# Retention and a gated feed-forward on one core: k's last heads on another queue, casts set among the steps, eight v buffers, and earlier loads

## The chip, the cores and the metric

The kernel runs on one core of a Trainium2 chip. The metric is the device time of one execution in microseconds. The kernel before was timed three times: 336.51 is the median, 334.05 the lowest and 338.14 the highest. One more execution was recorded by the hardware profiler; every row shown is from that one.

## The reference

Two stages follow each other, the first giving the second its rows:

```python
scores = (1 / sqrt(D)) * q @ k.T                     # per batch and head: 8 x 8, S = 576, D = 64
Dmat = where(i >= j, gamma[h] ** (i - j), 0)         # gamma[h] = 1 - 2 ** (-5 - h)
x = (scores * Dmat) @ v                              # then heads side by side: 4608 rows of 512
h = x @ w_in                                         # 512 -> 2048
out = (h * tanh(softplus(h))) @ w_out                # 2048 -> 512
```

All inputs and the output are float32 in memory; the kernel multiplies in bf16.

## The kernel before

The 576 positions of a batch are cut into four chunks of 128 and one of 64; the last chunks of two batches share one. That gives 36 chunks of 128 rows, and four chunks make a tile of 512 rows, nine tiles in all. The first two tiles hold the first chunk of each of the eight batches, which needs no earlier state. The other 28 chunks need the scores within the chunk and the sum of all earlier k and v, the state, which is carried per batch.

The order of the work is written out by hand: the scheduler is off, and each engine runs its instructions in the order in which the program states them. So an instruction that waits holds everything behind it on its engine. VectorE, ScalarE, GpSimd (POOL in the profile) and TensorE are four such rows; SyncE (SP), ScalarE and POOL also issue the loads. A DMA issue on a queue waits, besides for its buffer, for a semaphore that was last used eight loads before.

*Tile 0* (`f_cast(0, p)`, `f_transpose(0, p)`, `f_scores(0, p)`, `f_v(0, b)`, `f_out(0, b)`). A pair p is two of the eight heads. q is loaded in float32 into `stage`, a tile of the later type gT that is still free, by SP (heads 0 to 4) and ScalarE; k is loaded by POOL (`load_first_k`, L105), which casts on the way, into `kb0`; v by SP (L117). VectorE casts q pair by pair (L185), TensorE transposes q and k (L196), ScalarE copies them out (L200), TensorE makes the scores (L210), and VectorE multiplies them with the decay into the upper half of `stage` (L215). v is cast by POOL and ScalarE (L221). TensorE then gives the output (L235), which VectorE and ScalarE copy to xT (L238).

*The weights* come by POOL: w_in in two loads of 256 columns and three of 512 (L86), w_out in four (L89).

*Tile 1's q and k* are loaded by SP (`load_second_qk`, L112) into both halves of `stage`, pair by pair, q before k, sixteen loads of 128 KB. VectorE casts both (L185, two instructions a pair). All eight casts stand on VectorE ahead of the steps that follow.

*Tile 0's first feed-forward half* is `g1(0, f)`, f from 0 to 15: four matmuls of 128x512 (L369) and the activation on ScalarE (L371). Its second half, `g2_first`, sixteen groups of four matmuls (L395), is interleaved with tile 1's attention by a table: at step i, the letters T (transpose, L196, copies by VectorE for q and ScalarE for k, L200), S (scores), V (cast of v, ScalarE) and O (output) are run for pair or batch n, then one group. The tables before and after are in the change below. q's copy and k's copy of one pair read the same tile, and k's waits for q's.

*State scaling.* `f_state(t, b)` is a POOL multiplication of a first chunk's v with the inverse decay (L244), eight in all. `load_k0(b)` loads a first chunk's k once more, in the layout that the state needs (L248).

*From tile 2 on*, `load(n)` gives a chunk's q, k and v to POOL's queue (L262, or L266 for a shared chunk). The letters are P (VectorE scales q, L272), V (POOL scales v, L278), T (transposed by TensorE, or from chunk 16 on by SP's DMA, L290), S (scores, L300, and their mask, L304) and O (L350 and L355, copied by L359). `state` is L332, copied by L336. Tile 2's attention lies among the 24 steps of a loop over u that runs `g1(1, u)` and the first eight steps of `g2(1, ...)`, four steps to each j = u // 4; the others lie in the loop over t and i. `g2` is L384. Buffers for q and v in tiles 2 and later rotate over five (`io`, bufs = PF = 5), v with tile 0's and tile 1's v among them.

Of the kernel before, what the change touches and what calls it, by code (L numbers as in the profile page):

```python
# [10 lines left out]
F32 = mybir.dt.float32  # L11
# [6 lines left out]
def kernel(  # L18
# [18 lines left out]
    nc = tc.nc  # L37
    B, H, S, D = q.shape
    assert (B, H, S, D) == (8, 8, 576, 64)
    P = 128  # L40
    NP = H // 2
    d_model = H * D
    d_ff = moe_w_in.shape[1]
    nF = d_ff // P
    KC = d_model // P
    NCH = 4
    NPE = 16
    PF = 5
# [11 lines left out]
    N0 = 2 * NCH  # L60
# [4 lines left out]
    io = ctx.enter_context(tc.tile_pool(name="io", bufs=PF))  # L65
# [19 lines left out]
    def load_w_in(f0, n):  # L85
        nc.gpsimd.dma_start(out=w_in_t[:, :, ds(f0, n)], in_=w_in_r[:, :, ds(f0, n)])  # L86

    def load_w_out(i):
        nc.gpsimd.dma_start(out=w_out_t[:, ts(i, 4), :], in_=w_out_r[:, ts(i, 4), :])  # L89
# [2 lines left out]


    stage = gp.tile([P, nF, NCH * P], BF16, name="gT")
    raw = {0: (stage[:, 0:H, :].bitcast(F32),)}
    v0 = {}

    def rows(x, t, h):
        return x[ds(4 * t, 4), h, 0:P, :].rearrange("b (g r) d -> g b (r d)", r=4)
# [3 lines left out]
    def load_first_k(hs):  # L103
        for h in hs:
            nc.gpsimd.dma_start(out=kb0[:, h, :], in_=rows(k, 0, h))  # L105
# [7 lines left out]

    def load_first_v(t):
        for b in range(4 * t, 4 * t + 4):
            v0[b] = io.tile([P, H, D], F32, name="vraw")
            (nc.gpsimd if t else nc.sync).dma_start(out=v0[b], in_=v[b, :, 0:P, :].rearrange("h p d -> p h d"))  # L117

    for h in range(H):
        (nc.sync if h < 5 else nc.scalar).dma_start(out=raw[0][0][:, h, :], in_=rows(q, 0, h))  # L120
    load_first_v(0)

    zeros = consts.tile([P, 512], BF16)
# [13 lines left out]
                   allow_small_or_imprecise_dtypes=True)  # L137
    nc.gpsimd.iota(pos[64:P, 4:5], pattern=[[1, 1]], base=512, channel_multiplier=1,
                   allow_small_or_imprecise_dtypes=True)
    load_first_k(range(2, H))  # L140
    lg = [math.log(1.0 - 2.0 ** (-5.0 - h)) for h in range(H)]
    ex = consts.tile([P, 5, H], F32)
    for h in range(H):
# [26 lines left out]
    def keep_warm(n):  # L170
        for _ in range(n):
            nc.tensor.matmul(idle, lhsT=zeros[:, 0:P], rhs=zeros, start=True, stop=True)
# [5 lines left out]
    fst = {}  # L178

    def f_cast(t, p, copies):  # L180
        if p == 0:
            fst[t] = {"qb": first.tile([P, H, 4 * D], BF16, name="qb"),
                      "kb": first.tile([P, H, 4 * D], BF16, name="kb") if t else kb0, "vb": {}}
        for copy, name, src in zip(copies, ("qb", "kb"), raw[t]):
            copy(fst[t][name][:, ds(2 * p, 2), :], src[:, ds(2 * p, 2), :])  # L185

    def f_transpose(t, p, copies):
        if t == 0:
# [30 lines left out]
    def f_v(t, b, copy):  # L219
        vb = first.tile([P, H, D], BF16, name="vb", bufs=4)  # L220
        copy(vb, v0[4 * t + b])  # L221
        fst[t]["vb"][b] = vb
# [17 lines left out]
    def f_state(t, b):  # L240

        n = 4 * t + b
        v0s[n] = first.tile([P, H, D], BF16, name="v0s", bufs=B)
        nc.gpsimd.tensor_tensor(v0s[n], v0[n], gv[:, 0, :].unsqueeze(2).to_broadcast([P, H, D]), op=OP.mult)  # L244

    def load_k0(b):
        k0[b] = first.tile([P, H, D], BF16, name="k0", bufs=B)
        nc.gpsimd.dma_start(out=k0[b], in_=k[b, :, 0:P, :].rearrange("h p d -> p h d"))  # L248
# [3 lines left out]
    def load(n):  # L252
        if n >= n_chunks:
            return
        b, c = chunks[n]
        qr = io.tile([P, H, D], F32, name="qraw")
        vr = io.tile([P, H, D], F32, name="vraw")
        qks = io.tile([P, 2, H, D], BF16, name="qks", bufs=9)
        live[n] = {"q": qr, "v": vr, "qks": qks}
        for t, src in ((qr, q), (qks[:, 1], k), (vr, v)):  # L260
            if c < 4:
                nc.gpsimd.dma_start(  # L262
                    out=t, in_=src[b, :, ds(P * c, P), :].rearrange("h p d -> p h d"))
            else:
                for e in range(2):
                    nc.gpsimd.dma_start(  # L266
                        out=t[ds(64 * e, 64)],
                        in_=src[b + e, :, ds(512, 64), :].rearrange("h p d -> p h d"))
# [153 lines left out]
    def att(n, steps):  # L422
        if n >= n_chunks:
            return
        for step in steps:
            {"P": step_p, "V": step_v, "T": step_t, "S": step_s, "O": step_o}[step](n)

    dve, act, pool = nc.vector.tensor_copy, nc.scalar.copy, nc.gpsimd.tensor_copy


    for p in range(NP):
        f_cast(0, p, (dve,))
    keep_warm(8)
    for p in range(NP + 1):
        if p < NP:
# [3 lines left out]
            f_scores(0, p - 1)  # L439
    nc.scalar.activation(warm, pos[:, 0:1], AX.Mish)  # L440
    f_v(0, 0, pool)
    f_v(0, 1, pool)
    load_w_in(0, 256)
    load_w_in(256, 256)
    f_v(0, 2, pool)
    f_v(0, 3, act)
    for i in range(1, 4):
# [3 lines left out]
    load_second_qk()  # L451
    for i in range(4):
        load_w_out(i)
    for b in range(4):
        f_state(0, b)
    load_first_v(1)
    load_k0(0)
    make_masks()
    nc.vector.tensor_scalar(gq, gq, 1.0 / math.sqrt(D), None, op0=OP.mult)


    for p in range(NP):
        f_cast(1, p, (dve, dve))
    for f in range(nF):
        g1(0, f)
    load(N0)
    steps = {0: "T0", 1: "T1", 3: "S0", 4: "S1", 5: "T2", 8: "S2 T3", 11: "S3",
             12: "V0 V1 V2 V3", 13: "O0", 14: "O1 O2", 15: "O3"}
    for i in range(nF):
        for step in steps.get(i, "").split():  # L470
            n = int(step[1])
            if step[0] == "T":
                f_transpose(1, n, (dve, act))
            elif step[0] == "S":
                f_scores(1, n)
            elif step[0] == "V":
                f_v(1, n, act)
            else:
                f_out(1, n, (dve, act)[n % 2])
        g2_first(i // 4, i % 4)  # L480
    for b in range(4):
        f_state(1, b)
        if b == 1:
            load_k0(1)
        load(N0 + 1 + b)


    att(N0, "PV")
    for u in range(24):
        j, w = divmod(u, 4)  # L490
        if w == 0:
            if j < 3:
                load_k0(2 * j + 2)
                load_k0(2 * j + 3)
            if 0 < j:
                att(N0 + j, "PV") if j < 5 else None
                load(N0 + j + PF - 1) if j < 5 else None
            if 2 <= j < 6:
                att(N0 + j - 2, "O")
        elif w == 3 and j < 4:  # L500
            att(N0 + j, "T")
        elif w == 1 and 1 <= j < 5:
            att(N0 + j - 1, "S")
            state(N0 + j - 1)
        elif w == 2 and j < 5:
            state(N0 + max(j - 1, 0))
        if u < nF:
            g1(1, u)
        else:
            g2(1, u - nF)  # L510
    queued = [3 * NCH + PF]

    def more_loads(upto):
        for _ in range(2):
            if queued[0] <= upto:
                load(queued[0])
                queued[0] += 1

    for t in range(2, nT + 1):
        for i in range(nF):  # L520
            n, w = NCH * (t + 1) + i // 8 * 2, i % 8
            if t == nT:
                pass
            elif n == 3 * NCH:
                steps = {0: ((n, "T"), (n + 1, "PV")), 1: ((n + 1, "T"), (n, "K")),
                         3: ((n, "S"), (n + 1, "S"), (n + 1, "K")), 2: ((n + 2, "PV"),), 4: ((n + 3, "PV"),),
                         6: ((n + 1, "K"), (n, "O"), (n + 1, "O"), (n + 3, "K"), (n + 2, "T")),
                         7: ((n + 3, "T"),)}
                for m, step in steps.get(w, ()):
                    if step == "K":  # L530
                        state(m)
                        continue
                    att(m, step)
                    if step == "PV":
                        more_loads(m + PF)
            else:
                if w == 0:
                    att(n, "S")
                    att(n + 1, "S")
                    state(n + 1)  # L540
                if w in (0, 2):
                    att(n + 2 + w // 2, "PV")
                    more_loads(n + 2 + w // 2 + PF)
                elif w in (1, 3):
                    att(n + 2 + w // 2, "T")
                elif w == 4:
                    state(n + 3)
                    att(n, "O")
                    att(n + 1, "O")
                    state(n + 3)  # L550
                elif w == 6:
                    state(n + 3)
            if t < nT:
                g1(t, i)
            if t == 2:
                if i % 2:
                    g2(1, 8 + i // 2)
            elif t < nT or i < 12:
                g2(t - 1, i)
# [31 lines left out]
```

## Time and profile before

| | |
|---|---|
| median of 3 runs (lowest, highest) | 336.51 us (334.05, 338.14) |
| profiled execution, its time | 334.8 us |
| its span, from first to last instruction | 333.1 us |
| granted TensorE clock, mean over the span | 0.974 |
| busy: TensorE, weight loads, ScalarE, POOL, VectorE | 94%, 46%, 41%, 43%, 34% |
| first L369 of tile 0, of tile 1 | 19.65 us, 61.48 us |
| moved by DMA | 44.42 MB, mean 133 GB/s |

Times in rows count from the span's start. A row of the timeline gives start, duration, engine, line, operation and tiles; in square brackets stands how long the engine was idle before it and what ended that. "Busy" of TensorE counts matmuls from start to a modelled end, so it hides small gaps. DMA issues have their own view: how many, of what size, and the median time from issue to landing.

### The profile page before, as it was taken

What the parts mean: (1) busy time and instruction counts of PE and PEld (TensorE: products, weight loads), DVE (VectorE), ACT (ScalarE), POOL (GpSimd) and SP (SyncE); (2) the same over time, 40 slices, a digit from 0 to 9 for tenths busy, and PEclk for the clock granted to TensorE, in tenths of its full rate; (3) what the DMA queues carried; (4) which work ended last, traced back from release to release, by engine and by line L of the source; (5) the groups of instructions that cost most, each with busy time, mean ns of one, the idle gap of its engine ahead of it and who ended that gap; (6) DMA issues with size and microseconds to landing.
All of it is one profiled execution on the core that took longest, in us unless ns stands there. A gap on an engine that the chain in (4) does not pass through costs nothing.

```text
span 333.1 us, 5965 instructions
## 1 busy us (share of the span) xinstructions
PE 313.2 (94%) x2464; PEld 151.8 (46%) x2464; DVE 113.8 (34%) x160; ACT 137.8 (41%) x253; POOL 144.8 (43%) x178
## 2 busy tenths in 40 slices
PE   6889769999999999999969999999999999999995
PEld 2444324455445545444524444545454544444444
DVE  2641254354344342424251152525242432000111
ACT  5636213766276535342413433434344432333300
POOL 7593352999998856263708053627210000000000
PEclk9959979999999999999978999999999999999999
DMA  7999999999999999695999359798450400010031
GB/s 171 180 180 245 241 222 116 247 191 166 171 218 198 115 190 169 123 188 99 95 167 186 70 112 174 118 168 134 76 123 28 100 33 31 33 31 31 33 89 69
DMA packets 82490, 44.42 MB, mean 133 GB/s; under 512 B 65184, under 2 KB 74144, under 8 KB 82464
## 3 DMA queue, kind: packets, MB, share of 16 engines
q0 software_dynamic: 48336, 25.17, 56.5%
q1 hardware_dynamic: 33552, 18.36, 25.2%
q10 hardware_dynamic: 576, 0.52, 0.6%
q8 instruction: 19, 0.31, 0.4%
q14 instruction: 7, 0.06, 0.1%
HBM read 38.80 MB, written 9.44 MB: 145 GB/s over the span
## 4 chain that ended last, share of the span: by engine, by line
PE 78%; DMA 14%; DVE 3%; ACT 1%; issue 1%; POOL 1%; SPq 1%; DVEq 0%; ACTq 0%; POOLq 0%
PE hp L369 32%; PE ops L384 28%; DMA qkT<-qks 7%; DMA gT<-in_k_dram 6%; PE sc L300 2%; PE st L332 2%; PE hp L384 2%; PE hp L395 2%; DMA kb<-in_k_dram 2%; PE st L395 1%; ACT ssb L336 1%; PE sc L350 1%; PE hp L406 1%; PE sc L287 1%; PE sc L355 1%
## 5 line engine op out<-in xcount | busy, mean ns | idle before, releaser
L369 PE MATMUL hp<-xT,w_in_t 128*128 128x512 bf16 x576 | 147.8, 387 | 0.7 <-ACT xT L238 0.7
L371 ACT ACTIVATE gT<-hp 128x512 bf16<-128x512 f32 x144 | 86.1, 598 | 127.5 <-PE hp L369 125.7
L384 PE MATMUL ops<-w_out_t,gT 128*128 128x512 bf16 x464 | 118.9, 381 | 0.3 <-DVE res L414 0.3
L369 PEld LDWEIGHTS <-w_in_t 128*128 128x128 bf16 x576 | 54.1, 99 | 63.9 <-issue 5.4
L384 PEld LDWEIGHTS <-gT 128*128 128x128 bf16 x496 | 48.5, 98 | 59.5 <-issue 2.9
L414 DVE COPY res<-ops 128x512 f32<-128x512 f32 x30 | 20.8, 692 | 147.9 <-PE ops L384 144.4
L262 POOL DMA_DIRECT2D qraw<-in_q_dram x24 | 22.3, 930 | 53.8 <-DVE qks L272 51.9
L304 DVE TENSOR_TENSOR sm<-sc,mask 128x1024 bf16<-128x1024 f32 x28 | 33.2, 1217 | 12.4 <-PE sc L300 12.4
L278 POOL TENSOR_TENSOR vs<-vraw,gv 128x512 bf16<-128x512 f32 x28 | 30.4, 1098 | 12.4 <-PE sc L355 12.4
L336 ACT ACTIVATE ssb<-st,diag 128x256 bf16<-128x256 f32 x64 | 26.8, 470 | 17.1 <-PE st L332 16.3
L262 POOL DMA_DIRECT2D vraw<-in_v_dram x24 | 21.8, 907 | 9.0 <-ACT vb L221 6.7
L262 POOL DMA_DIRECT2D qks<-in_k_dram x24 | 21.7, 904 | 2.8 <-DMA w_out_t<-in_moe_w_out_dram 2.8
L359 DVE CAST xT<-sc 128x512 bf16<-128x512 f32 x28 | 18.2, 686 | 11.7 <-PE sc L355 11.6
L272 DVE TENSOR_TENSOR qks<-qraw,gq 128x512 bf16<-128x512 f32 x28 | 18.1, 683 | 0.0
L300 PE MATMUL sc<-qkT 64*128 64x128 bf16 x224 | 9.6, 221 | 3.3 <-DMA qkT<-qks 3.2
L350 PE MATMUL sc<-qkT,ssb 128*64 128x128 bf16 (+1 forms) x256 | 11.2, 215 | 0.0
L300 PEld LDWEIGHTS <-qkT 64*128 64x128 bf16 x224 | 6.4, 95 | 10.4 <-issue 5.9
L355 PE MATMUL sc<-sm,vs 128*64 128x128 bf16 x224 | 10.9, 219 | 0.0
L288 ACT COPY qkT<-sc 128x1024 bf16<-128x1024 bf16 x8 | 8.1, 1010 | 6.0 <-PE sc L287 5.9
L266 POOL DMA_DIRECT2D qraw<-in_q_dram x8 | 5.7, 714 | 11.3 <-DVE qks L272 11.3
L350 PEld LDWEIGHTS <-ssb 128*64 128x64 bf16 x256 | 7.8, 111 | 2.5 <-issue 2.5
L200 ACT COPY kbT<-sc 128x512 bf16<-128x512 bf16 x4 | 2.3, 585 | 16.0 <-DVE qbT L200 16.0
(81 smaller groups left out, 195.1 us busy)
## 6 DMA issues: line engine op xcount, KB each, us to landing
out_dram<-res SPq DMA_DIRECT2D x31, 256.0 KB, 3.2
vraw<-in_v_dram POOLq DMA_DIRECT2D x28, 256.0 KB, 6.7
qraw<-in_q_dram POOLq DMA_DIRECT2D x24, 256.0 KB, 5.8
qks<-in_k_dram POOLq DMA_DIRECT2D x24, 128.0 KB, 6.4
w_out_t<-in_moe_w_out_dram POOLq DMA_DIRECT2D x4, 512.0 KB, 22.1
gT<-in_q_dram SPq DMA_DIRECT2D x13, 128.0 KB, 7.4
w_in_t<-in_moe_w_in_dram POOLq DMA_DIRECT2D x3, 512.0 KB, 10.5
vraw<-in_v_dram SPq DMA_DIRECT2D x4, 256.0 KB, 7.2
```

The lines of the kernel that those rows point to most:

```text
L262: nc.gpsimd.dma_start(out=t, in_=src[b, :, ds(P * c, P), :].rearrange("h p d -> p h d"))
L272: nc.vector.tensor_tensor(live[n]["qks"][:, 0], live[n]["q"], gq[:, c, :].unsqueeze(2).to_broadcast([P, H, D]), op=OP.mult)
L278: nc.gpsimd.tensor_tensor(vs, live[n]["v"], gv[:, c, :].unsqueeze(2).to_broadcast([P, H, D]), op=OP.mult)
L300: nc.tensor.matmul(sc[:, e, p, :], lhsT=qk[r, 1, p, :], rhs=qk[r, 0, p, :], start=True, stop=True)
L304: nc.vector.tensor_tensor(sm.rearrange("p e n i -> p (e n) i"), sc.rearrange("p e n i -> p (e n) i"), m.unsqueeze(1).to_broadcast([P, 2 * ...
L336: nc.scalar.activation(ssb[:, :, e, :], st, AX.Copy, scale=diag[:, e:e + 1])
L350: nc.tensor.matmul(ot[ds(64 * e, 64), p, ds(i0, iw)], lhsT=st_sb[bb, cc][:, p, e, :], rhs=qk[:, 0, p, ds(i0, iw)], start=(i0 == 0 and p == ...
L359: nc.vector.tensor_copy(xts[t][:, :, ts(s, P)], ot)
L369: nc.tensor.matmul(hp, lhsT=w_in_t[:, c, ts(f, P)], rhs=xts[t][:, c, :], start=(c == 0), stop=(c == KC - 1))
L371: nc.scalar.activation(gts[t][:, f, :], hp, AX.Mish)
L384: nc.tensor.matmul(ops, lhsT=gts[t][:, f, ts(s, P)], rhs=w_out_t[:, f, :], start=(f == 0), stop=(f == nF - 1))
L414: copy(ot, ops)
```

## The change

- Heads 6 and 7 of tile 0's k leave POOL's queue. SP loads them in float32, ahead of tile 0's v, into the part of `stage` that pair 3's scores will take, and POOL casts them into `kb0`.
- The first 512 columns of w_in come in one load, between POOL's first and second cast of v.
- The v tiles rotate over eight buffers.
- Tile 1's v and the first `load_k0` go ahead of tile 0's state scaling; between the four scalings stand the loads of tile 2's chunks 8 to 11. They were issued after `g1(0)` and beside tile 1's scalings. Tile 1's scalings go into the loop over u, and chunks 12 to 15 are loaded behind them.
- Tile 1's casts of pairs 2 and 3 move into the table of steps, as letter C; S2 moves from step 8 to step 9.
- `load_k0` of batches 1 to 7 is spread: 1 before the loop over u, 2 and 3 at its end, 4 to 7 at steps 4 and 12 of tiles 3 and 4.

```diff
-    raw = {0: (stage[:, 0:H, :].bitcast(F32),)}
+    raw = {0: (stage[:, 0:H, :].bitcast(F32), stage[:, H:nF, :].bitcast(F32))}
...
-            v0[b] = io.tile([P, H, D], F32, name="vraw")
+            v0[b] = io.tile([P, H, D], F32, name="vraw", bufs=8)
...
+    for h in (6, 7):
+        nc.sync.dma_start(out=raw[0][1][:, h, :], in_=rows(k, 0, h))
     load_first_v(0)
...
-    load_first_k(range(2, H))
+    load_first_k(range(2, 6))
...
-            copy(fst[t][name][:, ds(2 * p, 2), :], src[:, ds(2 * p, 2), :])
+            if copy is not None:
+                copy(fst[t][name][:, ds(2 * p, 2), :], src[:, ds(2 * p, 2), :])
...
-        vr = io.tile([P, H, D], F32, name="vraw")
+        vr = io.tile([P, H, D], F32, name="vraw", bufs=8)
...
-        f_cast(0, p, (dve,))
+        f_cast(0, p, (dve, pool if p == 3 else None))
...
     f_v(0, 0, pool)
+    load_w_in(0, 512)
     f_v(0, 1, pool)
-    load_w_in(0, 256)
-    load_w_in(256, 256)
...
+    load_first_v(1)
+    load_k0(0)
     for b in range(4):
         f_state(0, b)
-    load_first_v(1)
-    load_k0(0)
+        load(N0 + b)
     make_masks()
...
-    for p in range(NP):
-        f_cast(1, p, (dve, dve))
+    f_cast(1, 0, (dve, dve))
+    f_cast(1, 1, (dve, dve))
     for f in range(nF):
         g1(0, f)
-    load(N0)
-    steps = {0: "T0", 1: "T1", 3: "S0", 4: "S1", 5: "T2", 8: "S2 T3", 11: "S3",
+    steps = {0: "T0", 1: "T1", 3: "S0 C2", 4: "S1", 5: "T2", 6: "C3", 8: "T3", 9: "S2", 11: "S3",
              12: "V0 V1 V2 V3", 13: "O0", 14: "O1 O2", 15: "O3"}
...
+            elif step[0] == "C":
+                f_cast(1, n, (dve, dve))
...
-    for b in range(4):
-        f_state(1, b)
-        if b == 1:
-            load_k0(1)
-        load(N0 + 1 + b)
+    load_k0(1)
...
-            if j < 3:
-                load_k0(2 * j + 2)
-                load_k0(2 * j + 3)
-            if 0 < j:
-                att(N0 + j, "PV") if j < 5 else None
-                load(N0 + j + PF - 1) if j < 5 else None
+            if 0 < j < 5:
+                att(N0 + j, "PV")
+                f_state(1, j - 1)
+                load(N0 + j + 3)
+            if j == 5:
+                load_k0(2)
+                load_k0(3)
...
-    queued = [3 * NCH + PF]
+    queued = [4 * NCH]
...
+            if t in (3, 4) and i in (4, 12):
+                load_k0(2 * t - 2 + i // 8)
```

## The prediction

> **What bounds the kernel now.** I read the page first, then TensorE's waits, then the timeline around the longest one.
>
> ```profile
> PE 313.2 (94%) x2464; PEld 151.8 (46%) x2464; DVE 113.8 (34%) x160; ACT 137.8 (41%) x253; POOL 144.8 (43%) x178
> ...
> PEclk9959979999999999999978999999999999999999
> ```
>
> TensorE is busy 94% of the span, so no other engine can be the bound on average; what can be won is its idle time and the slices where its clock is below 9. Those are slices 3, 5 and 6 (17 to 25 us, 33 to 50 us) and a pair past the middle. TensorE's waits say why:
>
> ```profile
> PE sc L210 <- ACT kbT L200: 4.8, 1, 4.8
> PE sc L300 <- DMA qkT<-qks: 3.2, 1, 3.2
> PE hp L196 <- DVE qb L185: 1.9, 1, 1.9
> ```
>
> Columns: total us, how often, the longest. The first row is one wait of 4.8 us before tile 1's first scores (L210). The timeline there, start and duration in us:
>
> ```profile
> 37.10 0.41 PE L196 MATMUL sc<-ident,qb 128*64 128x128 bf16 x8
> ...
> 38.55 1.03 PE L395 MATMUL ops<-w_out_t,gT 128*128 128x512 bf16 x4
> ...
> 40.32 0.43 DVE L185 CAST qb<-gT 128x512 bf16<-128x512 f32 x1 [1.81 <-DMA gT<-in_q_dram]
> 42.57 0.43 DVE L185 CAST kb<-gT 128x512 bf16<-128x512 f32 x1 [1.83 <-DMA gT<-in_k_dram]
> 42.92 1.28 DVE L200 COPY qbT<-sc 128x512 bf16<-128x512 bf16 x2
> 43.69 1.18 ACT L200 COPY kbT<-sc 128x512 bf16<-128x512 bf16 x2 [7.42 <-DVE qbT L200]
> ...
> 44.33 0.61 PE L210 MATMUL sc<-qbT,kbT 64*128 64x128 bf16 x8 [4.76 <-ACT kbT L200]
> 44.87 1.89 PE L395 MATMUL st<-w_out_t,gT 128*128 128x512 bf16 x4
> ```
>
> The transposes of pairs 0 and 1 had been done since 37.5. Their copies (L200) sat on VectorE behind the casts of pairs 2 and 3, which wait for SyncE's q and k loads, the last landing at 42.5. The wait is one of order on VectorE, not of data that TensorE needs then. And it costs more than itself, as the windows show (columns: busy of PE, PEld, DVE, ACT, POOL; granted clock; DMA share; GB/s):
>
> ```profile
> 42.00:44.00 2.00, 0.00 (x0) 0.00 (x0) 1.43 (x3) 0.31 (x1) 0.88 (x1) 1.00 1.24 233
> 44.00:46.00 2.00, 1.67 (x11) 0.78 (x12) 1.22 (x2) 0.86 (x2) 0.16 (x1) 0.56 1.09 258
> 46.00:48.00 2.00, 2.00 (x13) 0.69 (x12) 0.86 (x2) 0.00 (x0) 1.99 (x3) 0.59 1.08 209
> ```
>
> After the idle stretch the clock is near half until 47.6: from the scores at 44.33 to the transposes of pair 2 at 48.39 pass 4.06 us; the same two score groups (0.33 each, from 51.66 to 51.98) and two groups of four L395 (0.97 each) take 2.60 at full clock. So 1.46 us more.
>
> **The change, part by part.** *Casts of pairs 2 and 3 among the steps.* Nothing is removed; four casts of 0.43 go behind the first scores' multiply (C2) and behind T2 (C3). I follow the new order, with the durations above. TensorE ends its third L395 group at 39.57 and starts S0 there (its kbT copy would be ready at 37.6). VectorE: the multiply starts 0.44 after S0 and takes 1.23, so to 41.24; C2 to 42.10 (its data landed by 38.0); S1's multiply to 43.33; T2's qbT copy 0.69, to 44.02; C3 to 44.88 (its data landed by 42.5). TensorE: T2 at 39.57 + 2.60 = 42.17, just past C2; three L395 groups (0.97, 0.86, 0.86) and T2's own 0.57 bring T3 to 45.43, 0.55 past C3. So no wait of size is left: 0, at worst 1.0 (C2 caught by one POOL scaling of 1.1, less the 0.07). S2 one step later costs one more change between short and long matmuls, 0.1 (a group of four takes 0.97 after one, 0.86 otherwise). Part: -4.76 - 1.46 + 0.1 = -6.1. What is late next: T3, when pair 3's k lands after 43.0.
>
> *Two heads of k on SyncE ahead of v; their cast on GpSimd.* Removed: two L105 issues (0.59 each on POOL). Added: two 128 KB loads on SP ahead of four v loads, and one GpSimd cast, taken as its v cast of the same shape, 0.61. The last q load on SP lands at 9.3 (issued 3.73, 5.6 to landing), the second v at 12.8 (5.02 + 7.8): k's heads 6 and 7 lie between, and I take 10.9, since a q load follows the one before by 0.6 to 1.6. Cast until 11.6; TensorE needs it at 12.86. At 12.8 it would cost 0.6. The v casts follow: v moves up to 1.6 back, and the first weight load waits behind the first v cast on POOL. But TensorE starts L369 only at 19.65:
>
> ```profile
> 13.39 1.49 POOL L86 DMA_DIRECT2D w_in_t<-in_moe_w_in_dram  x2
> ...
> 15.43 2.24 POOL L86 DMA_DIRECT2D w_in_t<-in_moe_w_in_dram  x3
> ...
> 20.57 4.11 POOL L244 TENSOR_TENSOR v0s<-vraw,gv 128x512 bf16<-128x512 f32 x4
> ```
>
> *One 512-column weight load for two of 256.* Removed: one issue of 0.76. The pair landed at 17.2 and 19.9 (3.8 and 5.7 after issue), so a half takes 2.6 once the queue runs and 1.2 to start; the next 512 columns landed 3.2 later. One such load alone is then 1.2 + 3.2 = 4.4. Issued at 12.9, estimated from a first v at 12.3 and its cast, it is there at 17.3. Bounds: 16.7 if that v is no later and the cast of k alone holds it, 20.2 if it moves as two halves (1.2 + 5.2) and 0.9 later. I take the middle, so 0; worst 0.6. With the 0.6 before and 0.3 for later weights this part is 0, from -0.5 (a first landing of k sooner, as the queue is two loads lighter) to +1.5.
>
> *Loads ahead of the state scaling, eight v buffers.* The 4.11 us of L244 no longer stand before tile 1's v loads. That brings little: each of these issues waits for the eighth load before it on POOL's queue, as the 0.7 to 3.2 us idle before L117, L248 and L262 show, and the queue is fed all the while (245 GB/s from 24 to 40 us). SP's loads had 117 GB/s of it (eight loads of 128 KB in 8.97) and should keep them: 0. The last v of tile 1 landed at 50.2; its ScalarE cast is needed at 54.1 now. Eight buffers end the 6.7 us that POOL waited at L262 for ScalarE's v casts; loads of chunks 9 to 11 follow at once, 9 landing about 55.3 to 57 (chunk 8's v at 54.25, then 1.0 per 256 KB), needed from 59.3. Behind them on POOL stand the masks: 4 scalings x 1.05 and 12 issues x 0.9 put them at 58 to 59.4; VectorE's first use is 67.2 - 6.1 = 61.1. Covered by 1.7; without that cover S8's multiply and, after 1.7 more, O8 are late one for one. Later, each chunk's load runs one chunk less ahead; chunk 12's q is issued at 63.6 (masks at 59.4, a k load, two vs and one state scaling), lands 5.8 later at 69.4 and is multiplied at 72.7 (78.8 before). The k loads of batches 4 to 7 move from 72 to 79 us (with two that go to the end of the loop over u, 70 to 79 in all) into tiles 3 and 4, 0.9 of POOL each, where POOL idles (51.9 us before L262 in all). All 0, worst +1.
>
> [...] First the row: the scaling of gq (L459), 128x40, took 2576 ns at 19.19, ending with the first L244 scaling at 21.7, where ex (L144) took 175 for 128x5; yet the cast at 31.31 took its usual 0.43 beside a v issue from 31.27 on. [...] By the rows alone no scaling lies beside C2 or C3, and it stays -6.1.
>
> **Sum.** Profiled execution 334.8 (span 333.1 and 1.7 around it) - 6.1 = 328.7. The median of the runs shown, 336.51, lies 1.7 above that execution, the lowest 0.75 below; I forecast half of the 1.7 on top, 329.6.
>
> **Rivals.** *The second wait goes too, or comes again.* TensorE's other wait, 3.2 at L300, stands on a DMA transpose that took 14.0 to land where the median is 6.1:
>
> ```profile
> 168.00:171.60 3.60, 0.39 (x11) 0.22 (x12) 1.82 (x2) 0.00 (x0) 0.00 (x0) 0.85 1.07 143
> 171.50:177.50 6.00, 5.98 (x22) 2.32 (x23) 2.43 (x3) 0.70 (x2) 3.21 (x4) 0.51 1.20 195
> ```
>
> Its price is 3.2 idle and 6.00 x 0.49 = 2.9 at half clock, 6.1. The change does not touch that transpose; if the slow landing was chance and stays away, 329.6 - 6.1 = 323.5. For: one in 20 transposes. Against: the runs shown are no lower than the profiled one by more than 0.75.
>
> *Slower: the moved k loads beside the transposes.* Tiles 3 and 4 now get four POOL loads more on the engines that carry these transposes. A transpose has 14.0 - 3.2 = 10.8 us before TensorE waits. From one extra landing beyond that on, the gain is gone (335.7); with two it is 329.6 + 12.2 = 341.8. Against: a k load of 128 KB moved a landing by 0.4 to 0.9 at 75 to 77 us, and 6.1 + 0.9 is far from 10.8.
>
> *The wait moves to T3 or the weights.* If POOL's queue takes two thirds of the rate instead of half, pair 3's k lands near 46 and T3 starts 1.5 to 3 late, with some half clock: 332 to 335. For: margins of 0.07 and 0.55 only. Against: the equal share from 24 to 42 us, with POOL's queue never empty before either.
>
> *It does not do what it says:* the order on VectorE does change, so only a missed landing as above could undo it; with the first stage's worst, 335.6.
>
> **Chances.** Forecast 0.62; both waits gone 0.12; moved to T3 or the weights 0.14 (half of it still under 333.1); undone 0.04; slower 0.08. A measurement of this kernel tells about 1%, 3.4 us, from no change. Faster by over 1%: 0.62 + 0.12 + 0.06 = 0.80; within 1% 0.12; slower 0.08. The range 325.0 to 334.5 leaves out the slower case and most of the lowest; the forecast's own, the parts' ends and 2 for the spread of the runs shown, is 327 to 333.
>
> **What would show it.** Right: no wait of scores on kbT in TensorE's waits (L213 on L203 then), clock 9 in slices 5 and 6, tile 1's first L372 near 55.4 where L369 stood at 61.48, tile 0's still near 19.65, C3's k cast ending before T3. Wrong: TensorE waiting for casts (L188) or w_in_t, masks after 61, transposes landing past 10.8, or a gap of the same size at tile 1's V and O steps.

## Result, and the profile after

The changed kernel takes 324.73 us (median of four runs, 323.80 to 325.27) beside 337.09 for the kernel before (334.05 to 338.14): a ratio of 0.9645, with a 95% interval from 0.9576 to 0.9713. It is faster by some 12 us. Ratios, here and below, are of the runs' means and leave out runs that fell into a slower state (1.5% above the fastest of the same kernel), so they need not equal the quotient of two medians. The forecast of 329.6 had the direction right and missed the size; the time lies 0.3 below the range's low end of 325.0.

The profiled execution took 324.53 us against 334.8. In the code the lines behind the start have moved by 3: L369 is now L372, L395 is L398, L300 is L303, L332 is L335, the copies of the results L417 and their stores L420.

From the page of the kernel after, the busy times and the granted clock in 40 slices:

```profile
PE 308.4 (96%) x2464; PEld 150.3 (47%) x2464; DVE 111.3 (34%) x160; ACT 138.1 (43%) x253; POOL 143.8 (45%) x176
...
PEclk9879999799999999999999999999999999999999
```

The dips at 33 to 50 us and past the middle are gone. One is new, in slice 8 (56 to 65 us). TensorE's waits in the same trace (total us, how often, longest):

```profile
PE st L335 <- DMA qks<-in_k_dram: 2.3, 1, 2.3
PE hp L199 <- DVE qb L188: 2.2, 1, 2.2
PE st L238 <- DVE gT L218: 1.5, 2, 0.9
```

Both waits that headed this list before, 4.8 for kbT and 3.2 for the transposed q and k, are gone. A new one of 2.3 stands at the top.

The ledger, from the starts of the first-half groups in both traces, before minus after: the first group of tile 0 starts 0.61 sooner (19.65 to 19.04); the clock comes up 0.80 sooner behind it; from there to tile 1's first group 6.18 are won (it starts at 53.89 instead of 61.48); in tile 1's first four groups 4.00 are lost (8.25 us instead of 4.25); 0.31 are won up to tile 4; and 6.26 in tile 4. The sum is 10.16, and the last group is 10.15 sooner.

Where the casts went, in VectorE's and then in TensorE's own timeline of the kernel after:

```profile
38.53 1.22 DVE L218 TENSOR_TENSOR sm<-sc,dmask 128x1024 bf16<-128x1024 f32 x1 [1.40 <-PE sc L213]
39.67 0.42 DVE L188 CAST qb<-gT 128x512 bf16<-128x512 f32 x1
40.01 0.42 DVE L188 CAST kb<-gT 128x512 bf16<-128x512 f32 x1
...
42.07 0.42 DVE L188 CAST qb<-gT 128x512 bf16<-128x512 f32 x1
42.41 0.42 DVE L188 CAST kb<-gT 128x512 bf16<-128x512 f32 x1
```

```profile
38.09 0.40 PE L213 MATMUL sc<-qbT,kbT 64*128 64x128 bf16 x8
...
40.69 0.41 PE L199 MATMUL sc<-ident,qb 128*64 128x128 bf16 x8
...
43.95 0.41 PE L199 MATMUL sc<-ident,qb 128*64 128x128 bf16 x8
```

None of TensorE's rows has a bracket: it waits for no cast, and the casts end 0.3 and 1.1 us ahead of the transposes that read them.

The new wait, in the timeline from 50 us of the kernel after:

```profile
50.64 7.64 SPq L420 DMA_DIRECT2D out_dram<-res  x4
...
51.24 0.59 ACT L417 COPY res<-hp 128x512 f32<-128x512 f32 x1 [2.52 <-PE hp L398]
...
57.34 0.59 ACT L417 COPY res<-st 128x512 f32<-128x512 f32 x1 [3.63 <-DMA out_dram<-res]
...
58.06 0.32 PE L335 MATMUL st<-v0s,k 128*64 128x64 bf16 x8 [2.29 <-DMA qks<-in_k_dram]
...
60.44 2.90 PE L372 MATMUL hp<-xT,w_in_t 128*128 128x512 bf16 x8
```

TensorE's row blames a k load. ScalarE's row, 0.7 us earlier, shows what holds it: the copy of tile 0's fourth result needs one of three result buffers, and waits 3.63 us for the first store to give one back. That store, issued at 50.64, landed at 57.24, 6.6 us later; in the kernel before, where it was issued at 58.24, it took 3.2 (the last column; first the kernel after, then the one before):

```profile
out_dram<-res SPq DMA_DIRECT2D x1, 256.0 KB, 6.6
```

```profile
out_dram<-res SPq DMA_DIRECT2D x1, 256.0 KB, 3.2
```

Until the copy is done the one st tile is taken, and the first state (L335) writes there. Behind it the clock is low: the eight matmuls at 60.44 take 2.90 us, where eight take 1.89 at full clock. The windows from 54 to 65 us, after and then before, have the granted clock third from the end, ahead of DMA share and GB/s:

```profile
54.00:65.00 11.00, 8.62 (x52) 4.05 (x50) 1.91 (x4) 5.43 (x10) 10.69 (x16) 0.84 1.39 248
```

```profile
54.00:65.00 11.00, 11.00 (x96) 5.17 (x94) 5.09 (x7) 7.09 (x14) 8.75 (x10) 1.00 0.86 156
```

### The profile page after: what moved, and what is told of

Read it like the earlier page. It is cut to its first block, busy times and chain, and to the rows that moved or that the text cites. A ratio compares the mean times of both kernels' runs of the same rounds, so it can differ in the third digit from the quotient of the medians.

```text
span 322.8 us, 5961 instructions
## 1 busy us (share of the span) xinstructions
PE 308.4 (96%) x2464; PEld 150.3 (47%) x2464; DVE 111.3 (34%) x160; ACT 138.1 (43%) x253; POOL 143.8 (45%) x176
## 4 chain that ended last, share of the span: by engine, by line
PE 89%; DMA 3%; ACT 2%; DVE 2%; issue 1%; POOL 1%; ACTq 0%; DVEq 0%; POOLq 0%
PE hp L372 40%; PE ops L387 31%; PE st L335 3%; PE sc L303 2%; PE hp L398 2%; PE hp L387 2%; DMA out_dram<-res 2%; ACT ssb L339 2%; DMA kb<-in_k_dram 1%; PE sc L353 1%; PE sc L290 1%; PE hp L409 1%; PE sc L358 1%; PE st L398 1%; PE ops L398 1%
## 5 line engine op out<-in xcount | busy, mean ns | idle before, releaser
L372 PE MATMUL hp<-xT,w_in_t 128*128 128x512 bf16 x576 | 146.6, 385 | 0.8 <-ACT xT L241 0.7
L372 PEld LDWEIGHTS <-w_in_t 128*128 128x128 bf16 x576 | 54.0, 99 | 63.1 <-issue 3.0
L417 DVE COPY res<-ops 128x512 f32<-128x512 f32 x30 | 20.8, 692 | 143.8 <-PE ops L387 140.4
L339 ACT ACTIVATE ssb<-st,diag 128x256 bf16<-128x256 f32 x64 | 26.9, 472 | 17.1 <-PE st L335 16.2
L358 PE MATMUL sc<-sm,vs 128*64 128x128 bf16 x224 | 10.9, 219 | 0.0
L247 POOL TENSOR_TENSOR v0s<-vraw,gv 128x512 bf16<-128x512 f32 x8 | 9.4, 1180 | 0.0
L303 PEld LDWEIGHTS <-qkT 64*128 64x128 bf16 x224 | 6.3, 94 | 6.8 <-issue 5.9
L303 PE MATMUL sc<-qkT 64*128 64x128 bf16 x224 | 9.0, 217 | 0.0
```

The lines of the kernel that those rows point to most:

```text
L303: nc.tensor.matmul(sc[:, e, p, :], lhsT=qk[r, 1, p, :], rhs=qk[r, 0, p, :], start=True, stop=True)
L339: nc.scalar.activation(ssb[:, :, e, :], st, AX.Copy, scale=diag[:, e:e + 1])
L372: nc.tensor.matmul(hp, lhsT=w_in_t[:, c, ts(f, P)], rhs=xts[t][:, c, :], start=(c == 0), stop=(c == KC - 1))
L417: copy(ot, ops)
```

## Experiments

Twelve runs were made, of ten kernels, in three sittings on three chips, so times are compared within a sitting, and ratios to the kernel before across them. The kernel before, run once more, has no row in the table.

| kernel | median us | before, same sitting | ratio [95%] |
|---|---|---|---|
| casts alone | 331.45 | 337.69 | 0.9814 [0.9746, 0.9883] |
| casts and start | 323.01 | 337.69 | 0.9575 [0.9525, 0.9625] |
| whole change, four result buffers | 322.33 | 337.69 | 0.9541 [0.9479, 0.9603] |
| casts alone, eight small loads on SP | 324.36 | 335.92 | 0.9675 [0.9622, 0.9728] |
| casts alone, one q load held back | 324.42 | 335.92 | 0.9668 [0.9618, 0.9718] |
| casts and start, k on ScalarE's queue | 326.83 | 335.92 | 0.9711 [0.9653, 0.9768] |
| casts and start, four result buffers | 320.66 | 335.92 | 0.9564 [0.9524, 0.9605] |
| start alone | 329.66 | 334.87 | 0.9826 [0.9785, 0.9867] |
| whole change, again | 323.94 | 334.87 | 0.9679 [0.9629, 0.9730] |
| casts and start, again | 322.69 | 334.87 | 0.9623 [0.9587, 0.9659] |
| whole change, four result buffers, again | 322.13 | 334.87 | 0.9617 [0.9574, 0.9661] |

### The kernel before, once more

The file unchanged.

> The kernel before, unchanged, for a second profile. Its first one held a 3.2 us wait of the scores (L300) for a DMA transpose that landed after 14.0 us, worth about 6.2 us with the half clock behind it. If that slow landing belongs to the order of the loads, it is here again at the same chunk, 334 to 338 us. If it is chance, no landing passes 10.8 us and the time is near 329, or another transpose is the slow one.

It took 337.38 us. TensorE's waits:

```profile
PE sc L300 <- DMA qkT<-qks: 5.4, 1, 5.4
PE sc L210 <- ACT kbT L200: 5.2, 1, 5.2
```

The second wait is back, at the same chunk, behind the same pair of transposes: they land 9.7 and 16.2 us after issue (8.6 and 14.0 in the first trace). So the slow landing was not chance, and its absence from the kernel after asks for a cause.

### The casts alone

```diff
-    for p in range(NP):
-        f_cast(1, p, (dve, dve))
+    f_cast(1, 0, (dve, dve))
+    f_cast(1, 1, (dve, dve))
...
-    steps = {0: "T0", 1: "T1", 3: "S0", 4: "S1", 5: "T2", 8: "S2 T3", 11: "S3",
+    steps = {0: "T0", 1: "T1", 3: "S0 C2", 4: "S1", 5: "T2", 6: "C3", 8: "T3", 9: "S2", 11: "S3",
...
```

> The kernel before with only tile 1's casts of pairs 2 and 3 moved into the table of steps and S2 one step later. My theory: this alone takes the 4.8 us wait and the 1.5 us at half clock, 6.2 us less between tile 0's last and tile 1's first L369, and leaves the second wait as it was: 330 to 331 us, ratio 0.982. Rival, that the later wait also hangs on when the tiles run: 324 to 326 us and no wait at L300.

331.45 us, 0.9814. TensorE's waits, and the timeline where the new one stands:

```profile
PE sc L300 <- DMA qkT<-qks: 4.3, 1, 4.3
PE st L332 <- POOL v0s L244: 2.3, 1, 2.3
```

```profile
51.92 7.60 SPq L417 DMA_DIRECT2D out_dram<-res  x4
...
58.58 0.58 ACT L414 COPY res<-st 128x512 f32<-128x512 f32 x1 [3.60 <-DMA out_dram<-res]
```

The wait for kbT is gone by this edit alone, and the wait for a result buffer comes with it: the stores are issued six us sooner, and the first lands after 6.6 us. The wait at the first state (L332) is blamed on POOL's scaling here and on a k load in the kernel after; the copy's row is the same in both. The wait at L300 stays. In the profiled executions of this sitting, casts alone is 7.3 us ahead at tile 1's first group (it starts at 62.43 in the kernel before and at 55.16 here) and 3.3 from tile 2 on, since 4.0 are lost at the first state; a second wait that costs some 2 less then brings the spans to 330.4 and 335.7. So the expected ratio of 0.982 was met by other terms than the expected ones, which is luck: the 4.0 was not in the theory, and the second wait was to stay as it was.

### The casts and the start

As above, and the start part: the two k heads on SP, their cast on POOL, one weight load of 512 columns. Loads and states as before.

```diff
...
+    for h in (6, 7):
+        nc.sync.dma_start(out=raw[0][1][:, h, :], in_=rows(k, 0, h))
     load_first_v(0)
...
-    load_first_k(range(2, H))
+    load_first_k(range(2, 6))
...
+    load_w_in(0, 512)
     f_v(0, 1, pool)
-    load_w_in(0, 256)
-    load_w_in(256, 256)
...
```

> The casts part and the part at the start (k's heads 6 and 7 on SP, one weight load of 512 columns for two of 256), with the loads, the state scaling and the v buffers as before. Theory: 1.4 us less than the casts alone (0.6 from the earlier start, 0.8 from the clock coming up sooner), and no new wait before tile 2's first state, since the loads of chunks 9 to 11 do not crowd tile 0's stores: tile 1's first L369 near 54 and the next four groups at an unchanged distance of 4.25 us: 328.5 to 329.5 us if the transpose wait remains, 322 to 323 if it does not. Rival: the clock's 0.8 is chance, and it equals the casts alone.

323.01 us, 0.9575: 8.4 below casts alone in the same sitting. The row for the scores (L303 here) is gone from TensorE's waits; the pair of transposes lands in 5.8 and 8.3 us. And this kernel, without the earlier loads, is no slower than the whole change. The first store takes 4.9 us here, the copy waits 1.91 and TensorE 0.6. The expected 322 to 323 was met, but not by the terms named: tile 1's first group starts at 55.45, not near 54, so the clock's 0.8 is not there; between the profiled executions of casts alone and this kernel 3.0 us are won by tile 2 and 6.0 in tile 4.

### Four result buffers

```diff
-ot = op.tile([P, d_model], F32, name="res")
+ot = op.tile([P, d_model], F32, name="res", bufs=4)
```

On the whole change:

> The changed kernel with four buffers for tile 0's stored results instead of three. Theory: the 2.3 us wait at tile 2's first state (L335), which the trace puts down to a k load, is really ScalarE's fourth result copy waiting 3.6 us for the first store, 6.6 us to landing beside the loads of chunks 8 to 11; with a buffer more it goes, and its slow clock too: 4.0 us less, 320.5 to 321.5. Rival: the wait is for the k load as the row says, and the time stays at 324.7.

322.33 us, 0.9541; 320.5 to 321.5 was expected. The timeline:

```profile
51.81 4.39 SPq L420 DMA_DIRECT2D out_dram<-res  x4
...
55.26 0.58 ACT L417 COPY res<-st 128x512 f32<-128x512 f32 x1 [0.38 <-PE st L398]
...
56.88 0.32 PE L335 MATMUL st<-v0s,k 128*64 128x64 bf16 x8
```

The copy follows its matmuls, the state starts without a wait though the first store still took 5.4 us, and tile 1's first four groups take 4.25 us again instead of 8.25. That shows the buffer as the cause and 4.0 as its price in the trace. The medians give less: the ratio falls by 0.010 against the first measurement of the whole change, about 3.5 us, with intervals that overlap.

On the casts and the start:

> The casts and the start part with loads and states as in the kernel before, and four buffers instead of three for the second half's result. If the wait for a result buffer is what is left of the loss at tile 2's first state (0.6 us of TensorE's wait in the kernel with three), it goes, and the time is 0.6 to 1 below the 323.0 of that kernel: 322.2. If something else holds that place, the time stays at 323.0. Against the whole change with four buffers (322.3) it tells whether the earlier loads are worth anything once the buffer is there: equal within 0.5 if they are not.

The 0.6 us wait went as expected, but the ratio, 0.9564 beside 0.9575 in the other sitting, shows no gain that can be told from none. The 320.66 is not to be set against the 322.3 and 323.0 of another chip.

### Why the start part takes the second wait away

The timeline of the kernel before, around the transposes of tile 4's pair (156 us), and its DMA issues from 155.8 to 156.2 us (the last column is the time to landing):

```profile
155.71 0.93 POOL L262 DMA_DIRECT2D qraw<-in_q_dram  x1 [8.78 <-DVE qks L272]
...
155.91 2.89 SPq L290 DMA_TRANSPOSE qkT<-qks  x2
```

```profile
qraw<-in_q_dram POOLq DMA_DIRECT2D x1, 256.0 KB, 8.3
qkT<-qks SPq DMA_TRANSPOSE x1, 8.6
```

VectorE's scaling releases both, the transposes of one chunk and POOL's q load into the buffer it has read. At the earlier pairs SP issues 0.04 us after its wait ends and POOL 0.16 us later. At this pair, the seventh and eighth transposes, SP takes 0.47 us, and POOL is 0.20 us ahead. Just behind, from 156.4 to 156.6 us, there is one packet of 8 KB on the DMA queue q14, whose kind the profile gives as instruction (called a code load below):

```profile
q14 instruction: 1, 0.01, 15.4%
```

Counted in the trace, with its semaphore waits, the late transpose is SP's 80th instruction. In the fourteen recorded executions of this study the 80th instruction starts 0.46 or 0.47 us after the one before it has ended. With the start part SP has two more instructions ahead, and the 80th is then a semaphore wait ahead of the transpose; the next instruction waits another 2.0 us for VectorE's scaling anyway, so the gap is hidden in that wait. Hence three kernels, each shown as an edit of the kernel that its heading names.

*Casts alone, with eight loads of 256 bytes on SP and none of the start part:*

```diff
     load_second_qk()
+    dm = consts.tile([1, 8 * D], F32)
+    for i in range(8):
+        nc.sync.dma_start(out=dm[:, ts(i, D)], in_=q[0, 0, i:i + 1, :])
```

> The kernel with the casts alone moved, plus eight loads of 256 bytes each on SyncE's queue right behind tile 1's q and k loads, into a tile that nothing reads; nothing else of the change. What is asked: why the wait of 4 to 6 us ahead of tile 4's retention chunk (the line that reads the transposed q and k) is gone wherever the start part of the change is in. In each kernel without that part SyncE's seventh DMA transpose is issued 0.46 us after its wait ended, where the others take 0.04 us, and GpSimd's q load gets ahead of it. Theory A (the delay sits at a fixed place of SyncE's own instruction stream, and two more loads ahead move it off the transpose): here the seventh transpose is issued within 0.1 us again, its pair lands in 6 and 8 us instead of 9 and 15, the wait is gone, and the time is 331.45 - 4.3 = about 327. Theory B (it is the place of the loads themselves, k and the weights in the first 20 us, or the number of GpSimd's loads): nothing here changes it, the delay of 0.46 us and the wait of 4 us stay, and the time stays at 331.4 within 1.

```profile
151.37 2.88 SPq L290 DMA_TRANSPOSE qkT<-qks  x2
151.59 0.93 POOL L262 DMA_DIRECT2D qraw<-in_q_dram  x1 [8.78 <-DVE qks L272]
```

The transpose is first again (0.04 us behind its wait), the row for L300 is gone, and the ratio is 0.9675; the 327 expected is 0.968 of the kernel before in the sitting of casts alone. A trace without k on SP and without the single weight load has lost the wait. The 80th instruction is here a semaphore wait ahead of the sixth transpose: the gap of 0.46 us stands there, at 137.0 us, and the code load of 8 KB follows it at 139.1. This trace gives no landing time of the transposes. Not all of the gain over casts alone is this wait: the wait at the first state was 0.4 here, not 2.3, and why is not known.

*The start part with k's two heads on ScalarE's queue:*

```diff
-        nc.sync.dma_start(out=raw[0][1][:, h, :], in_=rows(k, 0, h))
+        nc.scalar.dma_start(out=raw[0][1][:, h, :], in_=rows(k, 0, h))
```

> The kernel with the casts and the start part, but heads 6 and 7 of tile 0's k on ScalarE's queue instead of SyncE's, so that SyncE's queue holds as many loads ahead of its transposes as in the kernel before. Theory A (position in SyncE's stream): the seventh transpose is late by 0.46 us again, its pair lands after 9 and 15 us, the wait of 4 us ahead of tile 4's chunk is back, and the time is 323.0 + 4.3 = about 327.3. Theory B (early k, fewer weight loads, number of GpSimd's loads): no wait, 323 within 1. The start of the first half should stay near 19 us either way.

```profile
149.93 0.93 POOL L265 DMA_DIRECT2D qraw<-in_q_dram  x1 [8.77 <-DVE qks L275]
150.13 2.88 SPq L293 DMA_TRANSPOSE qkT<-qks  x2
```

```profile
PE sc L303 <- DMA qkT<-qks: 3.5, 1, 3.5
```

The delay of 0.46 us is back on the transpose, POOL is ahead, the pair lands after 9.0 and 14.3 us, and TensorE waits 3.5. The ratio, 0.9711, is 0.0136 above the casts and start's, 4.6 us; 4.3 were expected. Everything else of the start part was in.

*Casts alone, with the q load held back:*

```diff
         live[n] = {"q": qr, "v": vr, "qks": qks}
+        if n == 27:
+            nc.gpsimd.memset(qr, 0.0)
```

> The kernel with the casts alone moved, and one more instruction: GpSimd clears the q buffer of one chunk (the one whose q load gets ahead of the late transpose) before its load, which puts that load some 0.5 us or more later, behind the transpose. Asked: whether it is the order of the two that makes the pair of transposes land late. If the order decides, the seventh transpose may still be issued 0.46 us late, but it and the eighth land in about 6 and 8 us as the other pairs do, the wait of 4.3 us is gone, and the time is about 327. If the late transposes have another cause (the same 0.4 us hiccup delaying something else), they still land after 9 and 15 us and the time stays at 331.4 within 1.

```profile
150.19 0.53 POOL L261 MEMSET qraw<- 128x512 f32 x1 [8.55 <-DVE qks L274]
150.63 2.67 SPq L292 DMA_TRANSPOSE qkT<-qks  x2
151.02 0.93 POOL L264 DMA_DIRECT2D qraw<-in_q_dram  x1 [0.30 <-POOL qraw L261]
```

The transpose is still 0.46 us late, but ahead of the load, and the pair lands in 5.8 and 6.8 us. The wait is gone; the ratio is 0.9668 (0.968 expected), with a wait at the first state of 1.5, not 2.3. So the delay alone does no harm: it costs when it lets the q load pass.

### The start alone, and the whole change beside its parts

> The start part by itself: heads 6 and 7 of tile 0's k on SyncE's queue, their cast on GpSimd, the first weights as one load; tile 1's casts stay behind tile 0's first half, loads and states as in the kernel before. The prediction gave this part nothing. If the shift of SyncE's instruction stream by two loads is what takes tile 4's wait away, this part alone is worth that wait: the wait of 5.2 us for ScalarE's cast ahead of tile 1's scores stays, the one for the transposed q and k goes, and the time is the kernel before less 5.4 to 6.3 (its wait there): a ratio near 0.983. If the two parts only work together, the ratio is 1.00.

0.9826, by that ratio 5.8 us under the kernel before (5.2 between the medians), with the casts where they were. TensorE's waits begin with

```profile
PE sc L213 <- ACT kbT L203: 6.1, 1, 6.1
```

and have no row for L303. The part to which the prediction gave nothing is worth as much in time as the one that was to bring everything: 0.9826 beside 0.9814.

Three kernels on one chip, for what the earlier loads cost:

> The whole change once more, for a comparison on one chip with the kernels beside it. Earlier, in separate sittings, it stood at 0.9645 of the kernel before and the kernel without the earlier loads at 0.9575, with intervals that overlap. If the earlier loads cost something (a result buffer comes free 2.3 us late where the first store meets them), this one is about 1.7 us slower than the kernel without them here too; if that was chance, they are within 0.5.

> The casts and the start part with loads and states as in the kernel before, beside the whole change on one chip: 1.7 us faster than it if the earlier loads cost what the two traces say, within 0.5 if not.

> The whole change with four result buffers, on the same chip: 2.4 to 4 us faster than the whole change if the wait for a buffer at tile 2's first state is the loss; then equal within 1 to the kernel without the earlier loads.

323.94, 322.69 and 322.13 us. The whole change is 1.25 behind the kernel without the earlier loads and 1.8 behind itself with four buffers; the wait at L335 is in its trace again (2.1). 1.7 and 2.4 to 4 were expected. The direction is that of the first sitting, but the intervals overlap both times. So a cost of about half a per cent is likely and not established. Three versions, casts and start with three or four buffers and the whole change with four, cannot be told apart and stand at 0.954 to 0.962, each a little ahead of the whole change in every comparison made.

## Why the prediction was right, and where it was wrong

*Casts among the steps: right, mechanism and size.* -6.1 was the sum; 6.18 were won between the clock's coming up and tile 1's first group. Pair 2's transposes were put at 42.17 and pair 3's at 45.43; less the 1.41 by which the kernel after was then ahead, that is 40.76 and 44.02, and they started at 40.69 and 43.95. VectorE was sooner than assumed, since multiply and casts overlap a little in its rows (C2 starts at 39.67, 0.08 before the multiply's 1.22 are over), so the margins were 0.3 and 1.1. The rival that moved the wait to pair 3's transposes needed k at 43 or later; the last k landed at 41.88.

*k's two heads on SP: the local working was right, what it moved was missed.* They landed at 9.37 and 9.85 where 10.9 was estimated, and their cast ended at 10.62, not 11.6. The first group of tile 0 started 0.61 sooner, just past the -0.5 end. The first weight load was issued at 12.04 and landed at 18.66, in 6.6 us instead of the 4.4 of the middle estimate, but within the bound of 20.2. The step that failed is a sentence in the first rival: "The change does not touch that transpose". The prediction followed the two loads through buffers, landings and casts, not through SP's instruction stream, where they moved a fixed hiccup by two places. The price was right (6.1, and 6.26 found); the condition was wrong (chance), and with it the 0.12.

*Loads ahead, and the wait for a result buffer: not nothing.* The masks were done at 57.3, sooner than the 58 to 59.4 expected, and nothing waited for them. The missed term is a consumer that the ledger of loads left out: tile 0's stores, which come six us sooner by the casts' own gain and meet the loads. The sum said nothing of result buffers. This term is +4.0 in the trace. It belongs to the casts' part of the sum as much as to the loads': casts alone, with the loads as before, loses the same 4.0, while casts and start is left with a wait of 0.6. That the loads in flight slow the stores is argued, not shown: the first store took 2.6 to 3.2 us where it was issued at 58 to 60 us, and 4.8 to 6.6 where it was issued at 50.6 to 52.3, and the DMA engines carried 248 GB/s from 54 to 65 us in the kernel after against 156 before. But the rate alone does not set it: from 51 to 57 us casts alone and casts and start carried 227 and 228 GB/s, and their first stores took 6.6 and 4.9. No kernel here took just these loads out of the stores' way, so what sets the store's time stays open.

*The sum.* 328.7 was forecast for an execution like the profiled one, which took 324.53: -0.6 for the start, -0.8 for the clock, -0.1 in the casts, +4.0 for the buffer, -0.3 between, -6.3 for the second wait make -4.1 of the -4.2. The 0.8 is no effect to count on: the fifth group starts at 23.7 in this trace, at 25.1 before, and at 24.8 in the whole change's second trace. The step of 0.85 to the median was too much; median and profiled execution of the kernel after are 0.2 apart. Two missed terms of opposite sign, 4.0 and 6.3, hid each other in part.

*Casts beside POOL's scalings: not shown.* No run shows the 1.0 that the prediction allows at worst for C2 caught by one POOL scaling. In the kernel after, the scalings nearest to the four casts start at 33.59 and 44.69 us, the casts lie from 39.67 to 42.83, and each took 0.42. The scaling of gq took 176 ns here, beside a load issue on POOL (18.79 us) and no scaling, and 2576 before, where it started 1.4 us ahead of a POOL scaling and ended within 0.1 us of it. What sets its time is not shown: it took 767 ns in the second trace of the kernel before and 527 in that of the whole change, beside load issues on POOL and no scaling. It moved no end.

## What to carry over

Any edit that adds or removes an instruction on a queue moves everything behind it in that engine's stream (with two loads more on SP, another instruction stood in the 80th place); where two engines are released by one event and the order of their issues matters, look at who is first, and by how little (0.2 us here), before calling a transfer untouched. When a stage is pulled forward, follow its outputs too: stores that come sooner meet other traffic, and the buffer that they hold is the next wait (here the first store landed after 6.6 us instead of 3.2, and 4.0 were lost). And where a wait's named releaser was done long before, look for a copy on another engine that waits for a store.

## What the hardware showed

- **A fixed gap in an engine's stream.** SP's 80th traced instruction started 0.46 or 0.47 us after the end of the one before it in all fourteen recorded executions (0.471 in the kernel before, 0.462 in the kernel after), with a code load of 8 KB behind it, 0.6 us where it was the transpose and 0.8 to 2.1 elsewhere. Whether the gap and the code load have to do with each other is not shown; that the place in the stream decides was shown by moving it, twice away from the transpose and once back. By letting the q load pass, the gap cost up to 6.3 us (6.26 in tile 4, before against after).
- **0.2 us of order, 6 us of time.** With POOL's q load 0.2 us ahead, the pair of transposes lands after 8.6 to 9.7 and 14.0 to 16.2 us (the kernel before, twice, and k on ScalarE's queue); 0.2 us behind, after 5.8 and 8.2 (the kernel after); 0.4 us behind, after 5.8 and 6.8 (the q load held back).
- **The clock can drop after a short idle time.** 2.29 us of TensorE idle up to 58 us were followed by matmuls at about two thirds of the full rate (eight in 2.90 us, against 1.89); over 54 to 65 us the granted clock was 0.84. The length alone does not decide: after the same kind of wait, 2.3 us in casts alone and 2.1 in the whole change's second trace, the granted clock from 54 to 65 us was 0.84 too, but after 1.5 us in the kernel with the q load held back it was 1.00, and after 3.5 us in the kernel with k on ScalarE's queue it was 1.00 as well (165 to 175 us). The mean over the span is 0.989 in both of these, as in casts and start, where TensorE waits 0.6 us and not at all at these two places.
